# Third round's last pair kept in SBUF, and the second round's side work carried into the expert blocks

## The chip, the core and the metric

One core of a Trainium2 chip runs the whole program in one launch. Its engines are TensorE (PE), VectorE (DVE), ScalarE (ACT), GpSimd (POOL) and SyncE (SP, which issues nearly all transfers); each works through its own instructions in the order in which the program lists them, and they wait for one another through semaphores. The metric is the device time of one execution in microseconds (us), smaller is better.

## The reference

A long convolution over the sequence, by FFT, followed by a two-level mixture of experts. There are 8 batches of 5056 tokens of 128 numbers; 16 experts (4 groups of 4) with 1024 hidden units.

```python
Xf = np.fft.rfft(x, n=2*S, axis=1); Hf = np.fft.rfft(h, n=2*S, axis=0)
y = np.fft.irfft(Xf * Hf[None], n=2*S, axis=1)[:, :S, :]      # (8, 5056, 128)
tok = y.reshape(-1, 128)                                       # 40448 tokens
g = argmax(tok @ w_group); e = argmax(tok @ w_expert[g])       # softmax weights of both
out[t] = weight * (relu(tok[t] @ w1[g, e]) @ w2[g, e])
```

## The kernel before

**The convolution** is a 2-step FFT written as matmuls. It runs in three rounds; each takes three of the nine sequences (H and 8 batches). A round has *stage 1* (`stage1`, 96 half steps) that fills the table `st`, and then *the groups* (`groups`): 79 frequency groups, taken as 40 pairs p = 0 to 39; pair 39 has only one group. For each pair there is a forward transform into PSUM (`forward`, L544), two products with H's spectrum on VectorE (`multiply`, L562: `y` and `m`), their sum (`add`, L596), the inverse transform (`inverse`, L612), a copy out of PSUM (L620 or L622) and stores to DRAM (`store`, L630 and L636: `zd`, and `ze` for the last rows). A group step takes two pairs and inverts the two before them, so pairs 38 and 39 of a round are inverted after its last group step, by a generator that is advanced piece by piece (`late`, `rest`).

**Side work** (`side`) of a round finishes what its groups left: 16 *lumps* of matmuls (L756 on tiles `zm`, two tiles to a lump, and then L770 on tiles `zt`, loaded from `zd` and `ze`); transposes into rows (`rows`); the gate's logits; the *gate math* (`gate_math`, L934 to L1026: some 25 small VectorE operations for each eighth of the round) which yields each token's place `pos`; and then 15 scatters of rows to `srt`, sorted by expert (`scatter`, L888, GpSimd's indirect transfers). Side work of round r runs beside the stage 1 and groups of round r+1; that of the third round beside the expert blocks. Rounds are numbered 0, 1, 2 in the code; "the second round's side work" is `side[1]`.

**The experts**: `ffn_steps` gives 8 steps for each block of 512 rows; I call them expert steps k = 0, 1, 2, ..., block j being steps 8j to 8j+7. A step has three matmuls of the first layer (`mm1`, L1410 to L1412) and three of the second on the hidden values of two steps before (`mm2`, L1430 to L1432). ScalarE makes the high part of the hidden values (L1415), VectorE the low part (L1418), and both split weights and rows (L1350, L1351). Block 0's rows are turned by VectorE first (`ffn_first`, L1366). Blocks 0 to 3 use rows of the first round alone (`tab_0`); block 4's rows (loads `xr<-srt`, L1314, issued at step 16 by `ffn_x`) need a table made from the second round's counts (`table_a`, seven pieces for a step) and wait until all scatters of the second round have landed. Block j's weights are asked for at step 8(j-2)+2 (`ffn_w`, L1343).

**What sets the order.** Everything on each engine runs in the order of one list, `main` (in `run`), into which `weave` mixes the side work: each entry of `main` has a weight, and side steps are put in so that the done share of the side's own weights follows the done share of the main weights between two marks. Only steps with weight let heavy side steps in; small ones are spread over the entries without weight that follow. Group pieces 7 and 11 weigh 2 each, expert steps k with k mod 8 = 2 or 6 weigh 1. The scatters stand in a queue (`sends`), popped one at a time by `send` at given places and by `drain` at step 15.

Before, side work of the second round ends ahead of step 2; pairs 38 and 39 are inverted at steps 0 and 1; the third round's first loads of `zm` and `zt` are asked for at step 7 and its side work starts at step 14. A lump asks for the loads of later lumps when it has used a tile up: the first lump (tiles 0 and 1) asks for tiles 3 and 4, and the second lump uses tiles 2 and 3.

Of the kernel before, what the change touches and what calls it, by code (L numbers as in the profile page):

```python
# [9 lines left out]
F32 = mybir.dt.float32  # L10
# [24 lines left out]
W = NU * D  # L35
# [5 lines left out]
T0, H0 = 1000, 2000  # L41
GP = 128
XT = 5
START2 = 14
LAST_FOLD = 44
NROW = 4
SQ = 32
GW = [0, 0, 0, 0, 0, 0, 2.0, 0, 0, 0, 2.0]
FW = [0, 0, 1.0, 0, 0, 0, 1.0, 0]
W_S1, W_END = 0.45, 2.5  # L50
SIDE1, SIDE2 = 14, 24
SIDE_AT = (14, 17, 20)
SLOTS = 56
LATE = 4
START1, END0 = 26, 24
NTA = 7
FILL, EMPTY = 12, 256
# [190 lines left out]
class Kernel:  # L248
# [238 lines left out]
    def groups(self, r):  # L487
# [6 lines left out]
        c0 = u0 * D  # L494
        w = nu * D
        cgs, hgs, ys, zs, minus = {}, {}, {}, {}, {}
        first = {}

        def load(p):
            if p >= NP:  # L500
# [69 lines left out]
        def product(p):  # L570
            px = forward(p)
            if r == 0 and p == 0:
                nc.vector.tensor_copy(
                    out=self.h0.rearrange("p (r d) -> p r d", d=HD),
                    in_=px[0:1, :, UH:UH + HD],
                )
                nc.vector.memset(hgs[p][0:1, 0, :], 0.0)
                nc.vector.memset(hgs[p][0:1, 2, :], 0.0)
            y = multiply(px, p, 0, "y", 4)
            self.send()  # L580
            yield
            m = multiply(px, p, 1, "m", 2)
            if p == 0:
                nc.vector.tensor_tensor(  # L584
                    out=m[0:1, 1, 0:w].rearrange("p (r u d) -> p r u d", r=2, u=nu), in0=taken(px[0:1], 1),
                    in1=self.h0.rearrange("p (r d) -> p r d", d=HD).unsqueeze(2).broadcast_to([1, 2, nu, HD]),
                    op=ALU.mult,
                )
            if r == 2 and p % 2 == 0 and len(self.sends) > 12:
                self.send()  # L590
            yield
            ys[p] = y, m

        def add(p):
            y, m = ys[p]
            self.mark["v"] = (nc.gpsimd if r == 0 else nc.vector).tensor_tensor(  # L596
                out=y[:, :, 0:w], in0=y[:, :, 0:w], in1=m[:, :, 0:w], op=ALU.add
            )

        def inverse(p):  # L600
            n = min(2, NG - 2 * p)
            if self.beside == "experts":
                pp, pz = None, [self.bank("pz"), self.ptr(1)][:n]
            else:
                pp = self.two()
                pz = [pp[:, 0], pp[:, 1]][:n]
            y, _ = ys.pop(p)
            for part in range(2):
                wt, k = (cgs[p + LP], 320 - part * 64) if p > 0 else (first[0], part * 128)
                for h in (0, 64):  # L610
                    for c in range(n):
                        nc.tensor.matmul(  # L612
                            pz[c][h:h + 64, 0:w], lhsT=wt[c * 64:c * 64 + 64, k + h:k + h + 64],
                            rhs=y[c * 64:c * 64 + 64, part, 0:w], start=part == 0, stop=part == 1,
                            tile_position=(c * 64, h),
                        )
            z = cx.tile([128, 2, W], F32, name="zs", bufs=3)
            if pp is None:
                for c in range(n):
                    self.mark["s"] = nc.scalar.copy(out=z[:, c, 0:w], in_=pz[c][:, 0:w])  # L620
            else:
                self.mark["s"] = nc.scalar.copy(out=z[:, 0:n, 0:w], in_=pp[:, 0:n, 0:w])  # L622
            zs[p] = z
# [41 lines left out]
        def step(k):  # L665
# [21 lines left out]
                        store(q)  # L687
            for p in (k, k + 1):
                if p < NQ:
                    add(p)  # L690
                    if p == k:
                        self.send()
            yield
# [18 lines left out]
            it = step(k)  # L712
            return [(w, lambda: next(it, None)) for w in GW]

        return pre(), [parts(k) for k in range(0, NQ + 2, 2)]

    def side(self, r):
        nc, cx = self.nc, self.cx
# [1052 lines left out]
    def run(self):  # L1771
        tc = self.tc
        with ExitStack() as ctx:
            self.pools(ctx)
            with ExitStack() as c2:
# [29 lines left out]
                for r in range(3):  # L1805
                    if r == 1:
                        add(self.share)
                    pre, steps = gr[r]
                    rest = late(r - 1) if r > 0 else []
                    n = len(s1[r][1])  # L1810
                    t0 = self.table_0()
# [25 lines left out]
                            add(advance(s1[r + 1][0] if r < 2 else early))  # L1837
                add(turn)
                add(lambda: self.ffn_first(0))
                rest = late(2)  # L1840
                ta, tq, tb, fill = self.table_a(), self.table_c(), self.table_b(), self.fill_rows()
                ahead = self.ffn_ahead()
                steps = [f for j in range(NW_MIN) for f in self.ffn_steps(j, (BLK, None) if j else None, NW_MAX)]
                for k, f in enumerate(steps):
                    for g in rest[LATE * k:LATE * k + LATE]:
                        add(g)
                    if k == 8 * (N0 - 2) - SIDE1:
                        mark["end", 1] = len(main)
                    if k == START2 - 7:
                        add(lambda: [side[2][0](q) for q in range(len(SIDE_AT))])  # L1850
                    if k == START2:
                        mark["start", 2] = len(main)
# [13 lines left out]
                        add(advance(ahead))  # L1866
                    if k < 4:
                        add(lambda q=(0, 2, 1, 3)[k]: self.ffn_w(1, (q,)))
                    add(f, FW[k % 8])
                    if k in (8 * (N0 - 2) - 1, 8 * (NA - 2) - 1):  # L1870
                        add(self.drain)
                    elif k < 8 * (NA - 2) and k % 8 not in (3, 4, 5, 6):
                        add(lambda: self.send("s"))
                    elif k >= 8 * (NA - 2) and k % 8 in (7, 0, 1, 2):
                        add(lambda: self.scatter_out(1, True))
# [37 lines left out]
```

## Time and profile before

| | us |
|---|---|
| median of 3 runs | 1610.87 |
| lowest, highest | 1610.49, 1612.48 |
| profiled execution, its own time | 1609.06 |
| its span in the trace | 1607.4 |
| TensorE busy | 1551.4 (97%) |
| VectorE, ScalarE, GpSimd busy | 1332.4, 992.8, 833.1 |
| mean granted TensorE clock | 0.994 |

A busy share tells of no bound by itself; the windows show the busy time and the granted clock (1.00 is 2.4 GHz, 0.50 is 1.2 GHz) for each stretch, and the timeline of an engine shows each gap with what ended it. Matmul ends are modelled and overlap, so distances between starts are the better measure of a matmul.

### The profile page before, as it was taken

The numbers are of one execution on the slowest core, as the hardware profiler recorded it, in microseconds if no ns is written. First come the engines' busy times: TensorE is split into PE (matmuls) and PEld (weight loads), VectorE is DVE, ScalarE is ACT, GpSimd is POOL, SyncE is SP. The second block draws the span as 40 slices with busy tenths as digits, with TensorE's granted clock in tenths as the row PEclk, the third lists the DMA queues.
The fourth block names the chain that finished last, engine by engine and source line by source line (L and its number), as shares of the span: only waits on it lengthen the run. The fifth ranks groups of instructions, "written<-read, shape, count | busy, mean of one in ns | idle before, by whom it ended". The sixth has DMA issues, their size and how long they took to land. (4 is left out here: it accounts for less than half of the span.)

```text
span 1607.4 us, 47247 instructions
## 1 busy us (share of the span) xinstructions
PE 1551.4 (97%) x16204; PEld 1215.8 (76%) x16204; DVE 1332.4 (83%) x2803; ACT 992.8 (62%) x2229; POOL 833.1 (52%) x799
## 2 busy tenths in 40 slices
PE   8998999998999989999999999999999999999997
PEld 8676855557766647887777777788887878889997
DVE  6654699885798987888888889999999998898886
ACT  5564544544555546666666666677777776666875
POOL 1453134344375664155656566367778853445445
PEclk9999999999999999999999999999999999999999
DMA  7797779979799987757776757587888886766566
GB/s 212 223 296 237 225 234 282 285 237 250 208 288 301 286 230 214 192 165 191 200 210 192 199 148 202 152 234 206 251 231 240 234 229 185 199 193 181 163 179 168
DMA packets 425346, 351.63 MB, mean 219 GB/s; under 512 B 255271, under 2 KB 362796, under 8 KB 425080
## 3 DMA queue, kind: packets, MB, share of 16 engines
q1 hardware_dynamic: 404472, 306.57, 68.6%
q0 software_dynamic: 20608, 41.79, 7.8%
q8 instruction: 134, 2.20, 0.6%
q14 instruction: 132, 1.08, 0.2%
HBM read 242.21 MB, written 106.53 MB: 217 GB/s over the span
## 5 line engine op out<-in xcount | busy, mean ns | idle before, releaser
L888 POOL DMA_INDIRECT srt<-rw,pos x320 | 341.4, 1067 | 329.8 <-DVE y L562 67.1
L1544 POOL DMA_INDIRECT out<-orow,at x176 | 185.8, 1056 | 181.3 <-ACT at L1542 117.0
L562 DVE TENSOR_TENSOR y<-pp,hg 128x768 f32<-128x768 f32 (+1 forms) x120 | 103.2, 860 | 53.1 <-ACT hg L552 32.2
L612 PE MATMUL pp<-y,cg 64*64 64x384 f32 (+1 forms) x1472 | 113.7, 440 | 4.8 <-DVE rw L1005 2.7
L1544 POOL DMA_INDIRECT out<-orow,sids x88 | 90.3, 1026 | 51.2 <-DVE lids L1559 17.5
L622 ACT COPY zs<-pp 128x768 f32<-128x768 f32 (+1 forms) x118 | 85.1, 722 | 51.2 <-PE pp L612 36.9
L544 PE MATMUL pp<-st,cg 64*64 64x192 f32 (+1 forms) x1556 | 114.1, 404 | 1.4 <-PE pp L612 1.3
L1415 ACT ACTIVATE h0h<-px 128x512 fp32r<-128x512 f32 (+1 forms) x109 | 63.8, 585 | 77.0 <-PE px L1412 76.9
L777 ACT COPY yT<-py 128x474 f32<-128x474 f32 (+1 forms) x96 | 44.3, 514 | 102.5 <-PE py L770 102.5
L457 DVE TENSOR_TENSOR st<-pp,odd 128x320 f32<-128x320 f32 x90 | 44.2, 491 | 72.2 <-ACT odd L456 71.9
L562 DVE TENSOR_TENSOR m<-pp,hg 128x768 f32<-128x768 f32 (+1 forms) x120 | 102.8, 857 | 0.0
L1418 DVE SCALAR_TENSOR_TENSOR h3l<-px,h3h 128x512 fp32r<-128x512 f32 (+1 forms) x111 | 74.1, 668 | 25.4 <-ACT h3h L1415 24.5
L1415 ACT ACTIVATE h2h<-px 128x512 fp32r<-128x512 f32 (+1 forms) x112 | 65.6, 586 | 45.3 <-PE px L1412 38.9
L1418 DVE SCALAR_TENSOR_TENSOR h0l<-px,h0h 128x512 fp32r<-128x512 f32 (+1 forms) x109 | 72.4, 664 | 24.1 <-ACT h0h L1415 22.1
L544 PEld LDWEIGHTS pp<-st,cg 64*64 64x64 f32 x1556 | 59.0, 133 | 43.0 <-issue 32.4
L596 POOL TENSOR_TENSOR y<-y,m 128x512 f32<-128x512 f32 x40 | 50.9, 1275 | 75.1 <-DVE m L584 42.0
L612 PEld LDWEIGHTS pp<-y,cg 64*64 64x64 f32 x1472 | 56.0, 133 | 43.4 <-issue 28.8
L756 PEld LDWEIGHTS py<-ig,zm 126*64 126x64 f32 x2048 | 74.5, 139 | 14.5 <-issue 8.4
L756 PE MATMUL py<-ig,zm 126*64 126x79 f32 x2048 | 82.6, 237 | 2.6 <-DMA zm<-zd 2.6
L1418 DVE SCALAR_TENSOR_TENSOR h2l<-px,h2h 128x512 fp32r<-128x512 f32 (+1 forms) x112 | 74.6, 666 | 9.7 <-ACT h2h L1415 6.8
L1415 ACT ACTIVATE h1h<-px 128x512 fp32r<-128x512 f32 (+1 forms) x111 | 65.1, 586 | 19.3 <-PE px L1412 17.1
L1415 ACT ACTIVATE h3h<-px 128x512 fp32r<-128x512 f32 (+1 forms) x111 | 65.0, 586 | 19.3 <-PE px L1412 17.4
(482 smaller groups left out, 5015.7 us busy)
## 6 DMA issues: line engine op xcount, KB each, us to landing
wr<-in_moe_w SPq DMA_DIRECT2D x186, 512.0 KB
zm<-zd SPq DMA_DIRECT2D x64, 378.0 KB
zd<-zs SPq DMA_DIRECT2D x62, 384.0 KB
cg<-in_c_g SPq DMA_DIRECT2D x102, 224.0 KB
xr<-srt SPq DMA_DIRECT2D x284, 64.0 KB
xt<-in_x SPq DMA_DIRECT2D x82, 160.0 KB
xt<-outd SPq DMA_DIRECT2D x45, 256.0 KB
hg<-hd SPq DMA_DIRECT2D x80, 128.0 KB
```

Of the source, the lines that this page charges most:

```text
L457: nc.vector.tensor_tensor(out=all_st[:, 0:2 * HALF, d], in0=even, in1=odd, op=ALU.add)
L544: nc.tensor.matmul(px[c * 64:c * 64 + 64, b, to], lhsT=k, rhs=data[:, of], start=begin, stop=i == len(steps) - 1 or p == 0 and i == 1, til ...
L562: self.mark["v"] = nc.vector.tensor_tensor(out=t[:, :, 0:w].rearrange("p t (r u d) -> p t r u d", r=2, u=nu), in0=taken(px, part).unsqueez ...
L596: self.mark["v"] = (nc.gpsimd if r == 0 else nc.vector).tensor_tensor(out=y[:, :, 0:w], in0=y[:, :, 0:w], in1=m[:, :, 0:w], op=ALU.add)
L612: nc.tensor.matmul(pz[c][h:h + 64, 0:w], lhsT=wt[c * 64:c * 64 + 64, k + h:k + h + 64], rhs=y[c * 64:c * 64 + 64, part, 0:w], start=part = ...
L622: self.mark["s"] = nc.scalar.copy(out=z[:, 0:n, 0:w], in_=pp[:, 0:n, 0:w])
L756: nc.tensor.matmul(pys[q][c:c + 64, col(n, u)], lhsT=zms[q][:, n % QB, k:k + 64], rhs=self.ig[:, 0:NH], start=n % QB == 0 and u == 0, stop ...
L777: nc.scalar.copy(out=self.yT[:, k:k + QB * c1], in_=pys.pop(q)[:, 0:QB * c1])
L888: ins = self.nc.gpsimd.indirect_dma_start(out=self.srt, out_offset=bass.IndirectOffsetOnAxis(ap=k["pos"][0:p, j:j + 1], axis=0), in_=k["rw ...
L1415: self.mark["s"] = nc.scalar.activation(out=hh, in_=p, func=AF.Relu)
L1418: nc.vector.scalar_tensor_tensor(out=hl, in0=p, scalar=0.0, in1=hh.bitcast(F32), op0=ALU.max, op1=ALU.subtract)
L1544: ins = self.nc.gpsimd.indirect_dma_start(out=self.a["out"], out_offset=bass.IndirectOffsetOnAxis(ap=ids, axis=0), in_=o, in_offset=None, ...
```

## The change

The last pair of the third round (p = 39) is no longer multiplied in the groups: its forward transform is copied from PSUM into a tile `kept` (on the `zm` buffers) by ScalarE, and `tail` makes y, m and their sum after expert steps 6, 7 and 9. Pair 38 is inverted at step 1 instead of 0, into the PSUM banks `ptr0` and `ptr1`; pair 39 at step 12 instead of 1, into `po[0]`; the stores of both pairs stand at step 13 instead of 2. The second round's side work ends ahead of step 6 instead of 2, where step 2 now counts 5 as a main weight, so 5 of 119.9 parts of it move beside block 0. The table for block 4 starts at step 7 instead of 3. The third round's first side loads stand at step 14 instead of 7 and its side work starts at step 18 instead of 14. Between steps 0 and 14 one or two scatters are sent after each step.

```diff
--- before.py
+++ after.py
@@ -41,17 +41,18 @@
 T0, H0 = 1000, 2000
 GP = 128
 XT = 5
-START2 = 14
+START2 = 18
 LAST_FOLD = 44
 NROW = 4
 SQ = 32
 GW = [0, 0, 0, 0, 0, 0, 2.0, 0, 0, 0, 2.0]
 FW = [0, 0, 1.0, 0, 0, 0, 1.0, 0]
 W_S1, W_END = 0.45, 2.5
-SIDE1, SIDE2 = 14, 24
+SIDE1, SIDE2 = 10, 24
+W_FIRST = 5.0
 SIDE_AT = (14, 17, 20)
 SLOTS = 56
-LATE = 4
+LAST, KEPT = {0: 3, 1: 1, 12: 1, 13: 6}, (6, 7, 9)
 START1, END0 = 26, 24
 NTA = 7
 FILL, EMPTY = 12, 256
@@ -494,7 +495,7 @@
         c0 = u0 * D
         w = nu * D
         cgs, hgs, ys, zs, minus = {}, {}, {}, {}, {}
-        first = {}
+        first, kept = {}, {}
 
         def load(p):
             if p >= NP:
@@ -576,6 +577,14 @@
                 )
                 nc.vector.memset(hgs[p][0:1, 0, :], 0.0)
                 nc.vector.memset(hgs[p][0:1, 2, :], 0.0)
+            if r == 2 and p == NQ - 1:
+                t = cx.tile([128, 2, W], F32, name="kept", tag="zm", bufs=3)
+                nc.scalar.copy(out=t, in_=px[:, :, 0:2 * UH])
+                kept[p] = t
+                self.send()
+                yield
+                yield
+                return
             y = multiply(px, p, 0, "y", 4)
             self.send()
             yield
@@ -591,6 +600,15 @@
             yield
             ys[p] = y, m
 
+        def tail():
+            for p in kept:
+                y = multiply(kept[p], p, 0, "y", 4)
+                yield
+                ys[p] = y, multiply(kept[p], p, 1, "m", 2)
+                yield
+                add(p)
+                yield
+
         def add(p):
             y, m = ys[p]
             self.mark["v"] = (nc.gpsimd if r == 0 else nc.vector).tensor_tensor(
@@ -600,7 +618,7 @@
         def inverse(p):
             n = min(2, NG - 2 * p)
             if self.beside == "experts":
-                pp, pz = None, [self.bank("pz"), self.ptr(1)][:n]
+                pp, pz = None, [self.po[0]] if p in kept else [self.ptr(0), self.ptr(1)]
             else:
                 pp = self.two()
                 pz = [pp[:, 0], pp[:, 1]][:n]
@@ -687,7 +705,8 @@
                         store(q)
             for p in (k, k + 1):
                 if p < NQ:
-                    add(p)
+                    if p not in kept:
+                        add(p)
                     if p == k:
                         self.send()
             yield
@@ -712,7 +731,7 @@
             it = step(k)
             return [(w, lambda: next(it, None)) for w in GW]
 
-        return pre(), [parts(k) for k in range(0, NQ + 2, 2)]
+        return pre(), [parts(k) for k in range(0, NQ + 2, 2)], tail()
 
     def side(self, r):
         nc, cx = self.nc, self.cx
@@ -1805,7 +1824,7 @@
                 for r in range(3):
                     if r == 1:
                         add(self.share)
-                    pre, steps = gr[r]
+                    pre, steps, tail = gr[r]
                     rest = late(r - 1) if r > 0 else []
                     n = len(s1[r][1])
                     t0 = self.table_0()
@@ -1837,16 +1856,17 @@
                             add(advance(s1[r + 1][0] if r < 2 else early))
                 add(turn)
                 add(lambda: self.ffn_first(0))
-                rest = late(2)
+                rest, past = late(2), 0
                 ta, tq, tb, fill = self.table_a(), self.table_c(), self.table_b(), self.fill_rows()
                 ahead = self.ffn_ahead()
                 steps = [f for j in range(NW_MIN) for f in self.ffn_steps(j, (BLK, None) if j else None, NW_MAX)]
                 for k, f in enumerate(steps):
-                    for g in rest[LATE * k:LATE * k + LATE]:
+                    for g in rest[past:past + LAST.get(k, 0)]:
                         add(g)
+                    past += LAST.get(k, 0)
                     if k == 8 * (N0 - 2) - SIDE1:
                         mark["end", 1] = len(main)
-                    if k == START2 - 7:
+                    if k == START2 - 4:
                         add(lambda: [side[2][0](q) for q in range(len(SIDE_AT))])
                     if k == START2:
                         mark["start", 2] = len(main)
@@ -1866,9 +1886,14 @@
                         add(advance(ahead))
                     if k < 4:
                         add(lambda q=(0, 2, 1, 3)[k]: self.ffn_w(1, (q,)))
-                    add(f, FW[k % 8])
+                    add(f, FW[k % 8] * (W_FIRST if k < 8 * (N0 - 2) - SIDE1 else 1.0))
+                    if k in KEPT:
+                        add(advance(tail))
                     if k in (8 * (N0 - 2) - 1, 8 * (NA - 2) - 1):
                         add(self.drain)
+                    elif k < 8 * (N0 - 2):
+                        for _ in range(1 + k % 2):
+                            add(lambda: self.send("s"))
                     elif k < 8 * (NA - 2) and k % 8 not in (3, 4, 5, 6):
                         add(lambda: self.send("s"))
                     elif k >= 8 * (NA - 2) and k % 8 in (7, 0, 1, 2):
```

## Rows read from the trace of the kernel before

**Rows 1.** Windows: stretch, busy us of PE, PEld, DVE, ACT, POOL, clock, DMA, GB/s.
```profile
585.00:590.00 5.00, 2.73 (x36) 1.11 (x32) 4.81 (x15) 2.42 (x7) 3.04 (x4) 1.00 0.66 182
...
595.00:600.00 5.00, 3.69 (x12) 1.26 (x12) 3.20 (x5) 3.36 (x8) 1.96 (x2) 0.79 0.92 239
...
600.00:605.00 5.00, 5.00 (x13) 3.89 (x14) 2.21 (x5) 2.15 (x4) 2.93 (x3) 0.53 0.96 198
...
660.00:680.00 20.00, 20.00 (x215) 16.58 (x215) 16.51 (x40) 12.15 (x26) 2.69 (x3) 1.00 0.68 197
```

**Rows 2.** TensorE's timeline: start, duration, engine, line, operation, [idle before <-releaser].
```profile
581.40 0.98 PE L816 MATMUL py<-ident,yT 128*128 128x128 f32 x7
...
583.33 0.51 PE L544 MATMUL pp<-st,ns 64*64 64x192 f32 x8
...
588.92 1.52 PE L612 MATMUL pp<-y,cg 64*64 64x384 f32 x16 [2.19 <-DVE rw L1005]
...
596.00 0.49 PE L1410 MATMUL px<-x0h,w0h 128*128 128x512 f32 x1 [1.62 <-ACT w0h L1350]
...
597.47 2.46 PE L612 MATMUL pz<-y,xt 64*64 64x384 f32 x8
...
599.86 0.79 PE L1410 MATMUL aux<-x0h,w0h 128*128 128x512 f32 x1
```

**Rows 3.** VectorE's timeline around the end of the groups.
```profile
579.52 0.40 DVE L956 TENSOR_TENSOR oh<-lg,go 128x240 f32<-128x240 f32 x1
...
586.10 0.15 DVE L987 TENSOR_SCALAR es<-es 128x15 f32<-128x15 f32 x1
...
587.83 0.95 DVE L562 TENSOR_TENSOR m<-pp,hg 128x768 f32<-128x768 f32 x1
...
590.49 1.81 DVE L596 TENSOR_TENSOR y<-y,m 128x768 f32<-128x768 f32 x2
...
594.07 0.70 DVE L1366 STREAM_TRANSPOSE xturn<-xr 128x512 f32<-128x512 f32 x1
```

**Rows 4.** The page's costliest groups (busy, mean ns | idle before): ScalarE's pair copy.
```profile
L622 ACT COPY zs<-pp 128x768 f32<-128x768 f32 (+1 forms) x118 | 85.1, 722 | 51.2 <-PE pp L612 36.9
```

**Rows 5.** GpSimd's timeline: first and last of eight in a row.
```profile
619.87 0.98 POOL L1544 DMA_INDIRECT out<-orow,at  x1 [2.02 <-ACT h0h L1415]
...
629.05 1.40 POOL L888 DMA_INDIRECT srt<-rw,pos  x1 [0.30 <-issue]
```

**Rows 6.** SyncE's timeline: block 4's rows, and the loads behind them.
```profile
633.58 1.95 SPq L1314 DMA_DIRECT2D xr<-srt  x4
...
636.99 1.38 SPq L1343 DMA_DIRECT2D wr<-in_moe_w  x2
...
638.47 0.85 SPq L734 DMA_DIRECT2D zm<-zd  x2
```

**Rows 7.** Waits of SyncE, 585 to 660: us in total, times, longest.
```profile
SPq L1314 <- DMA srt<-rw,pos: 6.7, 1, 6.7
```

**Rows 8.** SyncE's timeline, third round's stage 1: second load of zm.
```profile
365.95 0.32 SPq L734 DMA_DIRECT2D zm<-zd  x1
```

**Rows 9.** TensorE's timeline in the same stretch.
```profile
368.57 0.81 PE L439 MATMUL pp<-f,xt 64*64 64x80 f32 x32 [2.54 <-DMA xt<-in_x]
...
372.58 1.85 PE L756 MATMUL py<-ig,zm 126*64 126x79 f32 x24 [1.42 <-DMA zm<-zd]
```

**Rows 10.** TensorE's timeline in the first expert blocks.
```profile
609.86 0.39 PE L1410 MATMUL aux<-x0h,w1h 128*128 128x512 f32 x1
...
622.51 1.86 PE L756 MATMUL py<-ig,zm 126*64 126x79 f32 x48
...
624.31 1.03 PE L770 MATMUL py<-igt,zt 64*64 64x158 f32 x24
...
639.75 1.06 PE L826 MATMUL py<-yT,wge 128*32 128x512 f32 x8
```

**Rows 11.** Windows of 2 us, third round's stage 1: PE busy, clock, DMA, GB/s.
```profile
370.00:372.00 2.00, 1.16 (x18) 0.50 0.99 256
```

## The prediction

> **What bounds the kernel now.** I read the windows first, then TensorE's timeline wherever a window shows it idle, then the timelines of the engines named there. From the expert blocks on TensorE is the bound: 20.00 of 20 us busy in a window with lumps beside it [rows 1]. Time moves only where TensorE waits, or where its clock is low. The change touches one such place, the turn from the groups to block 0: in 585 to 590 TensorE is busy 2.73 us while VectorE is busy 4.81 [rows 1]. The reader is to see three things in TensorE's rows [rows 2]: pair 37's inverse starts 2.19 us late; the first matmul of block 0 starts at 596.00 after a wait for a split weight; step 1 starts at 599.86. Behind the 2.19 is VectorE: pair 38's m starts at 587.83 and lasts 0.95 [rows 3], though pair 38's forward transform ended at 583.33 + 0.51 = 583.84 [rows 2]. In between VectorE did gate math. The granted clock is 0.79 in 595 to 600 and 0.53 in 600 to 605 [rows 1]; of two levels, 1.0 and 0.5, that is 2.1 + 4.7 = 6.8 us at 1.2 GHz, after stretches of idling, and about 3.4 us lost.
>
> **Part 1, the turn comes earlier.** Removed from VectorE ahead of block 0's turn: y, m and sum of pair 39, three operations of about 0.9 us [rows 3]. Five parts of 119.9 of the second round's side work also move past the last group step. Following the weights, ahead of the turn there remain in VectorE's queue, after pair 38's m: three small gate operations (0.55, at some 0.2 each as L987), the sum of 38 (half of 1.81) and the gate math from L956 to L987. In the trace those stand between 579.52 and 586.25, 6.7 us of which 3.5 are y, m and two sums of pairs 36 and 37 [rows 3], so 3.25 us. The last eighth's seven transposes (0.98 us) move behind pair 37's inverse [rows 2], so pair 38's forward ends at about 582.9; y, one small operation and m end at 584.9, and the turn starts at 584.9 + 0.55 + 0.9 + 3.25 = 589.6 instead of 594.07 [rows 3]. From there to block 0's first matmul is 1.93 us, as now [rows 2, 3]: 591.5. Step 0 ends at 593.0, where it now ends at 597.47. Then pair 38's inverse, sixteen matmuls in 1.52 as pair 37's, and step 1 starts at 594.5 instead of 599.86 [rows 2]. The copy of pair 39 costs ScalarE 0.72 [rows 4] and lies behind the inverse of 36; if that cover went it would be 0.7 us.
>
> Steps 1 to 6 took 599.86 to 609.86 [rows 2, 10], of which 4.8 us at half clock; at the full clock they take 7.6. Step 6 then ends at 602.1. But TensorE now idles in one piece, from the end of the transposes to 591.5. They end at about 588.2: pair 39's forward about 1 us earlier than now, two inverses of 1.52 and the 0.98 [rows 2]. A gap of 2.54 us [rows 9] was followed by the low level, 0.50 in 370 to 372 [rows 11]; the 2.19 gap alone was not [rows 1, 2]. So I take one fall as before, 6.8 us long: step 6 ends at about 605.4. **Gain 4.5 us; 7.8 if the clock does not fall.**
>
> **Part 2, pair 39 beside the blocks.** Its inverse, eight matmuls, took 2.46 us at half clock [rows 2], so 1.2 at full clock at step 12; that is TensorE's and has no cover. Its y, m and sum (2.7 us) and the table for block 4 (some 24 small operations, which now start four steps later) both fall into steps 6 to 11; VectorE gets behind there. Bounds: nothing, if the two-step distance from hidden value to second layer absorbs it, to 3 us, the three products in full; I take 1.5, halfway, as no row is nearer to one end.
>
> **Part 3, the loads of the third round's side work.** The places of the second round's last eighth are now ready only at step 5, so its fifteen scatters start after step 6. Before step 15 GpSimd has these fifteen and two scatters of block 0's rows. Eight in a row now take 1.31 us from start to start [rows 5]. Seventeen: the last starts 21.1 us after the end of step 6 and ends at 22.5 (the last row took 1.40). From the end of the last scatter, 630.45, to the first load of block 4's rows, 633.58, there are 3.1 us [rows 5, 6], and SyncE spent 6.7 us on just that wait [rows 7]. So block 4's rows are asked for at 25.6, whatever TensorE does.
>
> The stores of pair 39, which SyncE now issues at step 13 after a wait for ScalarE's copy, hold up zt's first load (it reads what they write) and with it the first lump's second tile; TensorE may wait there too, but inside the 35.2 us below, which it doesn't set. The table's transfers stand there as well and are needed only before block 4's rows.
>
> Queued behind block 4's rows on SyncE are block 4's weights and, now, what the first lump asks for: it runs after step 18 instead of 14, so its loads stand behind step 16's instead of ahead. In the trace the first zm load behind block 4's rows comes 638.47 - 633.58 = 4.9 us after them [rows 6]: 30.5. How long such a load takes to land has no row at this place. Bounds: 3.1 us, a scatter's landing, and 6.4 us, zm asked for at 365.95 and the wait for it ended at 372.58 with the DMA share at 0.99 [rows 8, 9, 11]. I take the middle, 4.75, as neither row is the nearer: the scatter is far smaller, the other load stood among many. **Tile 3 lands at 35.2 (33.6 to 36.9).**
>
> The Trainium skill, DMA: Bandwidth & Descriptors, section Anatomy of one DMA, says that a wait on a semaphore is done by the issuing sequencer before dispatch, so what stands behind it is not begun; the 6.7 us agree. It also gives a fit for one transfer issued from GpSimd, 2.0 us plus bytes at 436 GB/s: 2.9 us for 378 KB, an estimate by which the sum below would be 1.85 us lower; the 6.4 us do not agree.
>
> When does TensorE want it? The second lump stands after step 22. From the end of step 6 to the end of step 22 with both lumps TensorE took 639.75 - 609.86 = 29.9 us [rows 10]. Add 1.2 for pair 39, take off what follows the first use of tile 3, half of the L756 row and the L770 row (0.93 + 1.03) [rows 10]: 29.2, or 30.7 with part 2's backlog. **TensorE waits some 4.5 us in the second lump (1.4 to 7.7)**, and step 22 with its lump ends 35.2 + 1.96 = 37.2 us after step 6 instead of 29.9: **a loss of 7.3**, in which parts 2's 1.2 and 1.5 are contained, since the load sets the time. An idle stretch of that length should bring the low clock again, another **3.4** as in the turn [rows 1].
>
> **Sum.** -4.5 + 7.3 + 3.4 = +6.2 us on the profiled execution's 1609.06: 1615.3. That execution is 1.8 below the median shown, so 1617 on the scale of the median. Landing at its bounds gives 1615.4 to 1618.8; with 1 us more for the pace of GpSimd and VectorE, the likeliest case's own range is 1614 to 1620.
>
> **Rivals.** (a) *One fall of the clock is missing*, after the turn or in the lump. For it: the low level did not follow every gap (2.19 us); against: both gaps are longer than 2.54. The sum becomes +2.8, 1613.7, about at the edge of what can be told.
> (b) *Faster: the load arrives in time.* The place is the second lump; it decides at an arrival before 29 to 31 us after step 6, which wants block 4's rows to be asked for at about 20 instead of 25.6, that is GpSimd taking 1.0 us for a scatter from start to start instead of 1.31, or the zm load not behind those rows. For it: a scatter's own duration is 0.98 [rows 5]; against: the 0.30 between two is in the row with no other cause. Then only part 1 and part 2 count: -4.5 + 1.2 + 1.5 = -1.8, 1609; without a fall of the clock -5.1, 1606; without the backlog also, 1604.
> (c) *The change does not do what it says*: block 0 does not start earlier, since gate math still stands ahead of its turn on VectorE (3.8 us by my count) and ScalarE's exponentials wait in the same chain. Then part 1 is worth nothing and the loads still come late: +10.7, 1621.6. Against it: VectorE was busy without a gap up to the turn, so what leaves its queue should show.
>
> **How the numbers follow.** A measurement of this kernel can tell about 0.2%, 3.2 us, from no change. Forecast 0.44 (slower). (a) 0.20: 0.06 slower, 0.14 within. (b) 0.30: 0.12 within, 0.18 faster. (c) 0.06, slower. Slower 0.56, within 0.26, faster 0.18. The range runs from 1606, which leaves out the best of (b), to 1621, which leaves out the most of (c); about 0.15 lie outside.
>
> **What would show it.** Right: block 0's first matmul some 4.5 us earlier against the end of the groups; y and m of pair 39 after step 6 with no wait for L1432 over 1 us; the scatters of the last eighth back to back at 1.3 us; SyncE's wait at L1314 for them; then L756 after step 22 with an idle of 2 to 8 us released by zm, and two stretches at half clock. Wrong: no idle ahead of that L756, or zm asked for ahead of block 4's rows; then the time falls to (b). A turn that starts as late as now against pair 37's inverse would mean (c).

## The result, and the profile after

| | before | after |
|---|---|---|
| median, us (4 runs each, same chip) | 1611.67 | 1631.81 |
| ratio to before, 95% interval | | 1.0123 (1.0099 to 1.0146) |
| profiled execution: its own time, span | 1609.06, 1607.4 | 1630.78, 1629.0 |
| mean granted TensorE clock | 0.994 | 0.989 |
| the same two kernels on another chip, medians | 1616.3 | 1631.91, ratio 1.0103 (1.0080 to 1.0127) |

The change costs 20 us; the forecast was 6. It is slower, as forecast, but 11 us beyond the end of the range. The experiments ran in three sets, each on one chip beside the kernel before: `tile3`, `late2`, `dens`, `e14`; then `phase`, `side1`, `best1`, `best2`; then `again`, `spread`, `best3`, `best4`. The medians of before in them are 1615.1, 1615.8 and 1616.3. Times of different sets are compared by their ratios to before.

**A common zero.** Single executions of one program reach the end of the groups at different times: in `before`, `late2`, `dens`, `phase` and `best2`, which are alike up to there (their traces come from several chips), pair 39's last forward matmuls start at 584.63, 590.31, 587.27, 588.68 and 590.06 us. So I set two traces against each other from that row on. What is left of the scatter goes with the length and the place of the clock's fall at the turn: `dens`, `phase` and `late2`, which are the kernel before up to step 14, agree with it to 0.02 us at step 0, and stand 2.3 ahead, 0.1 and 0.8 behind at step 14. So a difference of 2 or 3 us between two traces that arises between steps 1 and 7 is no result by itself.

TensorE's timeline of before (start, duration, engine, line, operation), and then the rows of after that decide:
```profile
584.63 0.51 PE L544 MATMUL pp<-st,ns 64*64 64x192 f32 x8
```
```profile
586.87 0.51 PE L545 MATMUL pp<-st,ns 64*64 64x192 f32 x8
...
594.86 0.50 PE L1429 MATMUL px<-x0h,w0h 128*128 128x512 f32 x1 [4.00 <-ACT w0h L1369]
...
611.58 0.17 PE L1071 MATMUL py<-nba_m,ones 128*128 128x16 bf16 x1 [2.93 <-DVE nba_m L1066]
...
619.33 1.51 PE L630 MATMUL pz<-y,xt 64*64 64x384 f32 x8
...
639.43 1.04 PE L775 MATMUL py<-ig,zm 126*64 126x79 f32 x24
...
647.40 1.85 PE L775 MATMUL py<-ig,zm 126*64 126x79 f32 x24 [6.93 <-DMA zm<-zd]
```
Block 0's first matmul stands 7.99 us behind the zero where it stood 11.37 [rows 2]: the turn is 3.4 us earlier. After it come a wait of 2.93 us for `nba_m`, the count for block 4's table, pair 39's inverse at the full clock, and 6.93 us of waiting in the middle of the second lump, for tile 3. VectorE's timeline shows why `nba_m` is late. From 604 on it works through its queue with hardly a gap (busy 4.90 of 5 us in 605 to 610), with expert work and pair 39's first product ahead of the count:
```profile
607.33 0.68 DVE L1437 SCALAR_TENSOR_TENSOR h1l<-px,h1h 128x512 fp32r<-128x512 f32 x1
...
609.73 0.95 DVE L563 TENSOR_TENSOR y<-kept,hg 128x768 f32<-128x768 f32 x1
...
611.22 0.31 DVE L1066 TENSOR_SCALAR nba_m<-cnta,iop 128x16 bf16<-128x16 f32 x1
```

The first matmul of each step, after less before, from the zero (negative is ahead; each entry is a difference of two starts in the timelines, less 2.24 for the zero):

| step | 0 | 7 | 8 | 14 | 22 | 24 | 32 (block 4) | 256 (block 32) | 544 (block 68) |
|---|---|---|---|---|---|---|---|---|---|
| after | -3.4 | -5.0 | -1.9 | +0.4 | -2.6 | +8.7 | +9.6 | +17.0 | +16.6 |

At step 22 after is ahead only because it hasn't yet run the first lump, which before runs behind step 14 (2.9 us); from step 14 to block 32 this evens out. So there are three losses. From step 7 to 14 it is 5.3 us. From 22 to 24 it is 11.3, of which 1.4 is side work in other places (`phase`, below, loses as much there without a wait), so 9.9 for the stall. What is left from step 14 to block 32 is 16.6 - 9.9 = 6.7 us, and no one place holds it. From block 68 to the end after takes 2.7 us more than before, with a wait of 2.40 us at 1486 that I can tie to no part of the change; in `again`, the same kernel, the end is 1.5 us shorter than in before, so I leave it out.

The windows of after (stretch, busy us of PE, PEld, DVE, ACT, POOL, clock, DMA, GB/s) show where the clock was low:
```profile
595.00:600.00 5.00, 4.69 (x22) 1.98 (x23) 3.31 (x12) 2.16 (x6) 1.84 (x2) 0.66 0.90 236
610.00:615.00 5.00, 3.42 (x11) 2.73 (x11) 4.70 (x15) 1.10 (x2) 3.49 (x3) 0.75 0.74 231
...
645.00:650.00 5.00, 2.60 (x36) 2.43 (x40) 0.00 (x0) 0.00 (x0) 0.00 (x0) 0.50 0.85 232
650.00:655.00 5.00, 5.00 (x29) 3.75 (x24) 0.69 (x1) 2.11 (x5) 0.00 (x0) 0.65 0.64 150
```
One fall follows each of the three waits. The one at the turn is short: 0.34 x 5 = 1.7 us lost, where before lost 3.4 [rows 1].

The third loss has no single row. These windows run from block 4's first matmul to block 32's, in before and in after:
```profile
655.67:1037.96 382.29, 377.61 (x2588) 299.66 (x2587) 328.38 (x706) 247.90 (x517) 201.24 (x188) 1.00 0.69 186
```
```profile
667.47:1057.18 389.71, 380.71 (x2594) 300.42 (x2593) 333.50 (x708) 249.00 (x520) 197.13 (x188) 1.00 0.65 182
```
After needs 7.42 us more for the same expert steps at full clock. Its idle time is 9.00 us (389.71 - 380.71), before's 4.68; the other 3.1 are in TensorE's busy time, of which 0.9 is work that has only changed its place: seven transposes of `yT` (168 matmuls on that tile against 161) that before runs ahead of block 4. One of the waits of after: VectorE's timeline ahead of it, and TensorE's row.
```profile
720.79 0.17 DVE L967 TENSOR_REDUCE es<-te 128x15 f32<-128x60 f32 x1
720.88 0.58 DVE L988 TENSOR_TENSOR oh<-go,eo 128x240 f32<-128x240 f32 x1
721.50 0.66 DVE L996 TENSOR_TENSOR_SCAN cs<-smask,oh 128x240 f32<-128x240 f32 x1
722.08 0.67 DVE L1437 SCALAR_TENSOR_TENSOR h0l<-px,h0h 128x512 fp32r<-128x512 f32 x1
```
```profile
722.80 0.49 PE L1451 MATMUL ptr<-h0l,w3h 128*128 128x512 f32 x1 [0.83 <-DVE h0l L1437]
```
Three gate operations of the third round stand in VectorE's queue ahead of a low half of h that TensorE wants next.

SyncE's timeline and its waits (us in total, times, longest) from 600 to 650, and GpSimd's first and last scatter of the second round's last eighth, all of after:
```profile
620.50 0.33 SPq L1142 DMA_DIRECT2D tabd<-tab  x1
...
628.76 0.28 SPq L1147 DMA_DIRECT2D tabr<-tabd  x1
636.88 1.97 SPq L1333 DMA_DIRECT2D xr<-srt  x4
...
641.22 0.84 SPq L753 DMA_DIRECT2D zm<-zd  x2
```
```profile
SPq L1142 <- DVE tab L1140: 8.7, 1, 8.7
SPq L1304 <- DMA tabr<-tabd: 4.9, 1, 4.9
...
SPq L1333 <- DMA srt<-rw,pos: 1.9, 1, 1.9
```
```profile
608.19 1.30 POOL L907 DMA_INDIRECT srt<-rw,pos  x1 [4.08 <-ACT w2h L1369]
...
634.35 1.01 POOL L907 DMA_INDIRECT srt<-rw,pos  x1 [0.30 <-ACT yT L796]
```
Tile 3 is asked for at 641.22 and lands at 647.40, 6.2 us later. SyncE stood 8.7 us for the table (VectorE computes it later than before), 4.9 for its way back through memory, and then only 1.9 for the scatters that I had made the whole reason.

### The profile page after: what moved, and what is told of

Same layout as the page of the kernel before. It is cut to its first block, busy times and chain, and to the rows that moved or that the text cites. A ratio compares the mean times of both kernels' runs of the same rounds, so it can differ in the third digit from the quotient of the medians.

```text
span 1629.0 us, 47242 instructions
## 1 busy us (share of the span) xinstructions
PE 1559.8 (96%) x16204; PEld 1221.1 (75%) x16204; DVE 1338.4 (82%) x2803; ACT 994.9 (61%) x2230; POOL 829.4 (51%) x799
```

## The experiments

All times are set against the kernel before on the same chip. "Ahead" and "behind" are TensorE's first matmul of a step from the zero above. Idle time is TensorE's from block 4 to block 32: 4.68 us before, 9.00 after.

**`again`, the changed kernel once more.** Nothing is changed.

> The changed kernel itself beside the kernel before on the chip of the other runs, so that the experiments can be set against it. By every theory the same as the first measurement, 1.009 to 1.015 of the kernel before, and in the trace the same steps measured from the last forward transform: 5 us ahead at step 7, 3 us lost at step 8, a wait of 6 to 8 us for tile 3 at the second lump.

1.0103 (1.0080 to 1.0127), median 1631.9 against 1616.3. In the trace the wait for `nba_m` is 2.92 us and the second lump's 5.67, a little under the 6 to 8 that were expected; TensorE is 9.5 behind at step 24 and 17.6 at block 32, with 9.22 us idle. The steps repeat; only the fall at the turn was a full one this time (2.50 + 0.65 + 0.25 = 3.4 us lost by the windows, 3.7 ahead at step 7 instead of 5.0).

**`tile3`: the tile early.**
```
-            if q >= nq:
+            if q >= nq or q in zms:
...
-            zm = cx.tile([RM, QB, W], F32, name="zm", bufs=3)
+            zm = cx.tile([RM, QB, W], F32, name="zm", **(dict(tag="m", bufs=2) if r == 2 and q == 3 else dict(bufs=3)))
...
-                        add(lambda: [side[2][0](q) for q in range(len(SIDE_AT))])
+                        add(lambda: [side[2][0](q) for q in range(len(SIDE_AT) + 1)])
```

> The changed kernel with one difference: tile 3 of the third round's side work is asked for at step 14 with tiles 0 to 2, into a buffer of its own (a free one of tag m), so it no longer stands behind the rows of block 4 on SyncE's queue. Theory Q (queue): the second lump's wait of 6.93 us goes and with it the clock fall behind it, 7 to 11 us, so 1621 to 1625 against 1631.8 for the changed kernel; what stays, 9 to 13 us over the kernel before, is not Q's. Theory S (the later and denser side work of the third round costs TensorE a little in every block, whatever the queue): the gradual loss of about 1.2 us per eighth in blocks 4 to 24 stays as it is. Rival R (the wait is not for the tile alone: zt or tile 2 comes as late): under 3 us gained, 1629 to 1632.

1.0087 (1.0066 to 1.0107), median 1626.3 against 1615.1. TensorE's rows of this kernel have no wait in the second lump:
```profile
642.47 1.86 PE L775 MATMUL py<-ig,zm 126*64 126x79 f32 x48
644.26 1.04 PE L789 MATMUL py<-igt,zt 64*64 64x158 f32 x24
```
From step 22 to 24 it loses 1.4 us, where after loses 11.3 and `again` 8.9. So the stall with its clock fall is worth 9.9 us in the trace of after and 7.5 in that of `again`. Theory Q holds for the stall, R is out. By the times it is less: from 1.0103 or 1.0123 to 1.0087, 2.6 to 5.8 us, a difference that is uncertain by some 5 us. TensorE then falls behind as in after: from step 14 to block 32 it loses 8.0 us, with 9.40 us idle. S holds too.

**`late2`: the third round's side work late, and nothing else.**
```
-START2 = 14
+START2 = 18
...
-                    if k == START2 - 7:
+                    if k == START2 - 11:
```

> The kernel before with one difference: the third round's side work starts at step 18 and not 14 (its first loads stay at step 7, its end where it was). No kept products, side work of round two as before. Theory Q alone (tile 3 is still asked behind block 4's rows): the second lump waits 3 to 7 us and a clock fall follows, so before plus 5 to 10, 1617 to 1622. Theory S as well: another 6 to 9 us comes gradually in blocks 4 to 24, so 1623 to 1630, near the changed kernel. Rival K (the loss comes from the kept products, the later inverse or the earlier turn): 1610 to 1614.

1.0079 (1.0056 to 1.0103), median 1629.0. Q and S both, without a kept product: the second lump waits,
```profile
648.65 1.85 PE L756 MATMUL py<-ig,zm 126*64 126x79 f32 x24 [4.41 <-DMA zm<-zd]
```
and TensorE goes from 6.3 behind at step 24 to 14.0 at block 32, idle 8.88. Rival K is out: this one constant brings most of the loss.

**`dens`: only denser.** `SIDE1, SIDE2 = 14, 28` instead of `14, 24` in the kernel before.

> The kernel before with one difference: the third round's side work ends four expert steps earlier (its start is as before), so it is spread over one weighted step fewer, as dense as in the changed kernel. Theory S in the form density: the loss of about 1.2 us per eighth shows here too, most of it caught up where the side work has ended, plus 3 to 9, 1614 to 1620. Theory S in the form phase (what counts is that lumps, transposes and gate rows fall on other steps of a block than in the kernel before, from the start): here the start is in phase and drifts, so under 4 us, 1611 to 1615. Theory Q: no difference, 1610 to 1613, and no wait of the second lump.

1.0021 (1.0006 to 1.0036), median 1617.7. No stall. TensorE goes from 2.3 ahead at step 14 to 2.6 behind at block 32, 4.9 us, with 7.24 us idle. On the way it was 7.6 behind at block 22, of which 4.6 came back by block 28, since its side work ends earlier. Theory S in the form density, in the lower part of its range; as a time, 3.4 us also fits the "under 4" of the form phase, and the next run decides between them.

**`phase`: only later.**
```
-START2 = 14
+START2 = 18
-SIDE1, SIDE2 = 14, 24
+SIDE1, SIDE2 = 14, 20
...
-                    if k == START2 - 7:
+                    if k == START2 - 11:
```
Tile 3 is loaded early as in `tile3`.

> The kernel before with the whole of the third round's side work four expert steps (half a block) later, start and end alike, so it is as dense as in the kernel before; tile 3 is asked for with the first three, so nothing stands behind block 4's rows. Theory P (phase: lumps, transposes and gate rows on the other half of a block): the gradual loss of 6 to 9 us over blocks 4 to 24 is there though the density is not raised; 1.003 to 1.007 of the kernel before. Theory D (density): no loss that grows, 0.998 to 1.002, as the side work ends later by the same half block. Either way no wait over 1 us ahead of the second lump.

1.0004 (0.9986 to 1.0021), median 1616.9. From step 14 to block 32 it loses 1.8 us (0.1 to 1.9 behind), idle 5.97. The time went as theory D said; P is out as the main cause and keeps the 1.8. With the 4.9 of `dens` that makes 6.7, as much as after loses beside the stall (`again` loses 7.3 by the same count, `tile3` 8.0); that the two simply add is not shown. Between steps 22 and 24, with no wait, this kernel loses 1.4 us, which I took off the 11.3 above.

**`e14`: the changed kernel with the third round's side work at its old place.**
```
-START2 = 18
+START2 = 14
-LAST, KEPT = {0: 3, 1: 1, 12: 1, 13: 6}, (6, 7, 9)
+LAST, KEPT = {0: 3, 1: 1, 10: 1, 11: 6}, (6, 7, 9)
...
-                    if k == START2 - 4:
+                    if k == START2 - 3:
```

> The changed kernel with the third round's side work started at step 14 as in the kernel before: the late inverse runs at step 10 and its store at step 11, and the first tiles are asked for at step 11. Products, copy and the second round's side work are as in the changed kernel. Theories Q and S together: the second lump comes before block 4's rows are asked for, and the side work has its old places, so about 17 of the 20 us go: 1611 to 1617. Q without S, or S without Q: 1619 to 1625. Rival L (the tiles, asked at step 11, land after step 14 and the first lump waits instead): a wait of 3 to 8 us at step 14, 1617 to 1625.

1.0041 (1.0026 to 1.0056), median 1622.0, by the ratios 10 us under `again`. The stall and the slow loss are both gone: 5.99 behind at block 4, 5.37 at block 32, idle 4.10. But 9.5 us were lost ahead of them, between steps 7 and 12:
```profile
614.46 0.17 PE L1071 MATMUL py<-nba_m,ones 128*128 128x16 bf16 x1 [2.93 <-DVE nba_m L1066]
...
619.95 2.72 PE L630 MATMUL pz<-y,xt 64*64 64x384 f32 x8 [2.48 <-issue]
```
The inverse at step 10 waits 2.48 us and then runs at half clock (2.72 where it took 1.51). The row does not name what it waited for, but VectorE's timeline does. The inverse reads y, and the sum that writes y ends 0.10 us before it starts:
```profile
618.90 0.95 DVE L614 TENSOR_TENSOR y<-y,m 128x768 f32<-128x768 f32 x1
```
ScalarE's copy of block 0's output out of the same bank had ended at 618.15. So this kernel made the wait itself: its inverse stands at step 10, and the sum behind step 9. Of the 9.5 us 3.1 are the wait for `nba_m`, as in after; the rest is the inverse, its wait and the clock. As a time, 1622.0 lies in the range given for one theory without the other; by the trace both hold, and the loss stands in a place that no forecast named. Rival L is out.

**`side1`: the second round's side work alone.**
```
-SIDE1, SIDE2 = 14, 24
+SIDE1, SIDE2 = 10, 24
+W_FIRST = 5.0
...
-                    add(f, FW[k % 8])
+                    add(f, FW[k % 8] * (W_FIRST if k < 8 * (N0 - 2) - SIDE1 else 1.0))
```
and the sends of the first steps as in the change.

> The kernel before with the second round's side work alone ended at expert step 6 (start of the table's operations and sends moved with it), nothing kept, third round as before. Theory V (the wait of 2.9 us ahead of step 8 comes from the table's counts being emitted four steps later, behind expert work on VectorE): the wait for nba_m is here too, 2 to 4 us, and the time is 1.001 to 1.004 of the kernel before. Theory M (it comes from the kept products on VectorE): no wait over 1 us there, 0.998 to 1.001, as the gate operations of the last eighth leave the way of the turn.

1.0019 (1.0008 to 1.0029), median 1619.4 against 1615.8. The wait is here with nothing kept:
```profile
622.07 0.17 PE L1053 MATMUL py<-nba_m,ones 128*128 128x16 bf16 x1 [2.18 <-DVE nba_m L1048]
```
TensorE is 0.2 behind at step 7, 3.1 at step 12 and 2.8 at block 32. Theory V; M is out as the cause, though with the kept products in the same queue the wait is 0.75 us longer. And the turn comes only 0.9 us earlier (step 0) where the whole change brings 3.4: the products of pair 39 have to leave VectorE's way as well.

**`best1`: products behind step 0, inverse at step 4, third round at its old place.**
```
-START2 = 18
+START2 = 14
-LAST, KEPT = {0: 3, 1: 1, 12: 1, 13: 6}, (6, 7, 9)
+LAST, KEPT = {0: 3, 1: 1, 4: 1, 5: 6}, {0: 3}
...
-                pp, pz = None, [self.po[0]] if p in kept else [self.ptr(0), self.ptr(1)]
+                pp, pz = None, [self.ptr(0)] if p in kept else [self.ptr(0), self.ptr(1)]
...
-                    if k == START2 - 4:
+                    if k == START2 - 7:
...
-                    if k in KEPT:
+                    for _ in range(KEPT.get(k, 0)):
```

> The changed kernel with the third round's side work at its old place (loads at step 7, start at step 14), the kept pair's products and sum queued on VectorE right behind step 0, where it idles, and the late inverse at step 4 in the bank ptr0. If the causes named so far are all (tile 3 behind block 4's rows, the third round's side work moved by half a block, kept products ahead of the table's counts), the 3.4 us that the turn comes earlier are kept and little is lost: 0.996 to 1.000 of the kernel before. If the table's counts wait whatever the kept products do (theory V): 1.000 to 1.003.

1.0009 (0.9995 to 1.0023), median 1616.6. Within 0.8 us of before from step 9 to block 68 (0.4 ahead at block 32), idle 3.77. 4.3 us ahead at step 3, it pays 1.3 for the inverse at step 4 and 2.4 for `nba_m`:
```profile
618.66 0.17 PE L1071 MATMUL py<-nba_m,ones 128*128 128x16 bf16 x1 [2.20 <-DVE nba_m L1066]
```
with the clock at 0.66 in the 5 us behind it. Theory V's number.

**`best2`: as `best1`, second round's side work as before** (`SIDE1, SIDE2 = 14, 24`, `W_FIRST = 1.0`, no extra sends; products two behind step 0, one behind step 1).

> As the last, but the second round's side work ends at step 2 as in the kernel before, so the one change is the pair copied out of PSUM, its products behind step 0 and its inverse at step 4. Theory V: no wait for the table's counts, 0.996 to 0.999. Theory M: like the last one. Rival: with the gate operations of the last eighth back in the first two steps, the products at step 0 hold up the first expert rows, 1.000 to 1.003.

0.9998 (0.9981 to 1.0015), median 1615.3. No wait for the count. The turn is only 1.5 us earlier, and that goes later, in step 4 and at the second lump (0.1 behind at step 22). Between the two forecasts; nothing is won by the kept pair alone.

**`best3`: as `best1`, the count's product some eight operations of the table later on TensorE.**
```
-        for _ in range(8):
+        for _ in range(16 if name == "nba" else 8):
```

> The version with the third round at its old place and the kept products behind step 0, with TensorE's product of the table's counts put some one to two steps behind VectorE's operation that it waits for. Theory V (that product stands in TensorE's queue ahead of step 8 while VectorE is late): the wait of 2.2 us and its clock fall go, 3 to 4 us, so 0.996 to 0.999 of the kernel before. Rival: the wait moves with it (VectorE has not caught up by step 9), 0.999 to 1.002.

0.9994 (0.9977 to 1.0011), median 1614.9. The wait shrinks and the clock stays full in the 5 us behind it:
```profile
613.17 0.17 PE L1071 MATMUL py<-nba_m,ones 128*128 128x16 bf16 x1 [0.83 <-DVE nba_m L1066]
```
```profile
613.00:618.00 5.00, 4.83 (x24) 4.05 (x24) 4.86 (x17) 2.96 (x6) 3.78 (x5) 1.00 0.87 241
```
TensorE is 3.2 ahead at step 8 where `best1` is 0.5, and still 2.9 ahead at block 32. Theory V in the trace, though the wait did not go altogether; the time is the same as before, in the range of the rival (0.999 to 1.002).

**`spread`: as `tile3`, gate operations spread wider.**
```
-                at += [(t + 4.02 + 3.3 * k / (NMATH + REST2), advance(ops), True) for k in range(NMATH + REST2)]
-                at.append((t + 7.4, lambda o=o, s=sends: self.sends.extend((8 * r + o, f) for f in s), True))
+                at += [(t + 4.02 + 5.0 * k / (NMATH + REST2), advance(ops), True) for k in range(NMATH + REST2)]
+                at.append((t + 9.1, lambda o=o, s=sends: self.sends.extend((8 * r + o, f) for f in s), True))
```

> The changed kernel with tile 3 asked for early, and the 38 gate operations of each eighth of the third round spread over 5.0 side units and not 3.3. Theory G (in blocks 4 to 31 TensorE waits for the low halves of h because bursts of gate operations stand ahead of them on VectorE): TensorE's idle time there falls from 9.4 us to 4 to 6.5, and the kernel is 3 to 6 us faster than the one with the early tile alone: 1.004 to 1.007 of the kernel before. Rival T (the waits come from the transposes, lumps and copies themselves): idle time within 1 us of 9.4, 1.008 to 1.010.

1.0033 (1.0016 to 1.0051), median 1621.8, by the ratios 8.7 us under `tile3` (by the steps of the trace 4 to 5). From block 4 to block 32:
```profile
659.53:1045.74 386.21, 377.20 (x2595) 301.42 (x2593) 330.86 (x709) 249.83 (x520) 200.36 (x188) 1.00 0.67 184
```
3.9 us more than before, where `tile3` needs 7.9; from step 14 it is 3.1 against 8.0. Theory G has the time, a little better than it said, but idle time as a whole stays at 9.01 us, as T said. Its content changes: TensorE's waits for low halves of h fall from 5.8 us in eleven waits to 1.5 in three, as G said (3.0 in before), and in their place stand 3.8 us in six waits of up to 0.6 us for ScalarE's copy `yT` (1.3 in two in `tile3`) and one of 1.7 for a gate operation. What falls beside them is TensorE's busy time, 380.8 to 377.2 with the same 2595 matmuls at the same clock; 1.5 of it is in the rows of L1451, the matmuls that read a low half (89.91 to 88.40). I read this as waits too short to be counted as idle, which sit in the modelled matmuls.

**`best4`: `best3` with the same spread.**

> The last version with the third round's gate operations spread over 5.0 side units as well. Theory G: idle time of TensorE in blocks 4 to 31 falls from 3.8 us to 1 to 3, so 1 to 3 us off the last one: 0.994 to 0.998 of the kernel before. Rival: at the old places the bursts cost little, and spread they meet other steps: within 1 us of the last one.

0.9999 (0.9983 to 1.0016), median 1616.2. Idle time rises from 4.23 to 8.11 us, and 2.5 ahead at block 4 becomes 0.1 behind at block 32. Here too the waits for low halves fall (3.0 to 1.5 us), but TensorE now waits 4.5 us in seven waits for `yT`, where it waited none. Spread is no good in itself: from the old places it meets other steps. The rival had the mechanism, though the price in the trace is 2.6 us; the time shows no difference.

## Why the prediction was wrong

The step that failed most is a term put at nothing: the third round's side work was priced by its loads alone, and moving it cost TensorE some 7 us more, spread over the expert blocks. From the zero the forecast was +7.2 us (the 6.2 of the sum, and 0.98 of the gain that lies ahead of the zero), and the profiled run ended at +19.4. Of the 12.2 between them 2.4 came before block 4, 7.4 from block 4 to 32, and 2.4 behind that, of which the cause stays open.

**Part 1, the turn: right.** Forecast 4.5 us earlier, of which 0.98 by transposes that leave the way of pair 38's forward transform, so 3.5 from the zero; measured 3.4. The seven transposes did move (589.88 in after, behind the inverse), but eight others now stand ahead of pair 38's forward transform (583.53 to 584.55); whether the 0.98 came in the time can't be seen, since executions that are alike up to there scatter by up to 5.7 us. The clock fell once, as taken, but cost 1.7 us in one profiled run and 3.4 in the other, so TensorE was 5.0 and 3.7 us ahead at step 7. Rival (c) is out.

**Part 2, pair 39 beside the blocks: right kind, undersized.** The inverse was forecast at 1.2 us, and step 12 grew by 1.5. The backlog was taken at 1.5 us between 0 and 3, out of sight behind the wait for tile 3. TensorE lost 3.1 us at step 8 and 0.5 in the steps behind it. The step that failed here is the choice of who waits: I looked at the second layer's matmuls, and none of them waited over 1 us. The one that waits is the small product of the table's counts. The prediction had noticed that the table starts four steps later, and counted its operations as load on VectorE. It did not ask which engine has an instruction queued that needs one of them: L1071 stands in TensorE's order ahead of step 8, and everything behind it waits. `side1` shows the wait without the kept products; `best3` moves the product and the wait falls to 0.83.

**Part 3, the late tile: right, undersized.** Forecast: block 4's rows asked for 25.6 us after the end of step 6, tile 3 landed at 35.2, a wait of 4.5. Measured from 607.13, where step 7 of after begins: 29.75, 40.3 and 6.93, inside the 1.4 to 7.7. Two terms were short. The rows were late because two chains ran late together: 17 instructions took GpSimd 28.2 us and not 22.5 (22.4 by its own 1.31 and 1.40), with gaps between the scatters; and the table, which I had put aside as "needed only before block 4's rows", held SyncE until 635.0 (636.88 less the 1.9 for the scatters) by its own waits of 8.7 and 4.9. By these rows the scatters alone would have brought all of the 4.15 us of delay and the table alone 2.3; neither was tried alone. The load took 6.2 us from issue to landing: of my two bounds, the 6.4 of the same transfer (6.6 by its own two rows [rows 8, 9]) was the price and the 3.1 of a scatter was not. The fit in the Trainium skill, DMA: Bandwidth & Descriptors, section Anatomy of one DMA, which is for transfers issued from GpSimd, gives 2.9 us for 378 KB, an estimate; the 6.2 of this load, issued by SyncE, does not agree. The wait and its low clock were worth 9.9 us in after and 7.5 in `again` (against `tile3` in the trace) where I had 4.5 + 3.4 = 7.9, so this size was right within what two runs of one kernel differ by; the tile came 5 us later than forecast, and TensorE asked for it 2.6 us later.

To block 4's first matmul the sum was thus +7.2 against +9.6, both from the zero, an error of sizes and of who waited, not of the path.

**What was not in the sum, and failed most: 6.7 us of side work in worse places.** The prediction gave the third round's side work no price beyond its loads. It took the 20.00 of 20 us in 660 to 680 [rows 1] to mean that lumps and gate operations lie beside the blocks at no cost of their own, wherever they stand. They don't. From step 14 to block 32 the same work costs 1.8 us more when it is moved half a block and kept as dense (`phase`), 4.9 when it starts at its old step and ends four steps earlier (`dens`), and both together 6.7 in after and 8.0 in `tile3`, with idle times of 6.0, 7.2, 9.0 and 9.4 us. At its old places it costs nothing more, whatever else was changed (`e14`, `best1`, `best3`: idle 3.8 to 4.2). Part of the way is shown: VectorE's gate operations ahead of h's low halves. Spreading them takes the waits for low halves from 5.8 to 1.5 us and `tile3`'s 8.0 us down to 3.1 (`spread`). Why one weighted step fewer, 2 per cent of density, moves so much is not settled. The same spread at the old places brings a loss (`best4`), so how many operations stand together is not the whole of it; that it is where they fall is what fits best, and no run isolates it.

**The forecast and the rivals.** The likeliest case was the right one in sign, and in mechanism up to block 4. Rival (b) did not come about, nor (a): the clock fell three times, not twice. No rival let the loss go on after block 4, which is why the range ended at 1621.

## What to carry to other kernels

A later start for side work with a fixed end moves and packs every later piece of it too, and here a full engine paid for that in many short waits, part of which no idle time shows; price the new places, not only the moved loads. For each operation that starts later, list the engine whose queue holds its first reader, small products of a table included: that queue stops as a whole. Of two bounds for a transfer, take the row of the same transfer under load.

## What the runs showed of the hardware

TensorE's idle time in the trace seems to miss short waits: `tile3` and `spread` have 9.40 and 9.01 us of idle in the same expert steps, with the same 2595 matmuls at a clock of 1.00, and differ by 4.0 us, 3.6 of it in busy time.

Short waits can bring the half clock: it was granted after waits of 4.00, 2.93, 2.20 and 2.18 us (mean clock 0.66 to 0.75 in the 5 us around them), though not after 0.83 in `best3`, nor after the 2.19 of before [rows 1, 2], nor after the 2.93 of `e14` (1.00 in 614 to 619), where it came only behind the next wait, of 2.48 us (0.51 in 620 to 625). So the length of a wait alone did not decide it. A fall costs nothing while the engine waits, and then the work behind it runs at 1.2 GHz: behind the wait of 6.93 us another 3.0 us went. The Trainium skill, TensorE: Matmul & The Clock Gate, section HAM oscillation — how this bites in real kernels, describes this for waits on loads, and the windows at 645 to 655 agree.
